# One more Strassen pair in a fused attention and feed-forward kernel, with two loads issued later

## The chip, the cores and the metric

The kernel runs on one core of a Trainium2 chip. The core has five engines that work side by side, each through its own queue in order: TensorE (PE in the profile; its weight loads are PEld), VectorE (DVE), ScalarE (ACT), GpSimd (POOL) and SyncE (SP), which here only issues transfers. Transfers issued by SP run in the DMA queue q1, those issued by POOL in q0. The time is that of one execution on the device in microseconds (us); the figure for a kernel is the median of its runs.

## The reference

Two steps. First attention with a local window and a few global keys, for 4 batches of 8 heads, 768 positions and 64 features:

```python
scores = scale * np.matmul(q, k.transpose(0, 1, 3, 2))
keep = is_global | is_local            # key < 8, or 0 <= query - key < 96
bias = -slopes[:, None, None] * dist   # distance, capped for the global keys
a = softmax(np.where(keep, scores + bias, -1e9))
x = matmul(a, v)                       # as 3072 tokens of 512 features
```

Then a feed-forward layer over the 3072 tokens, with 1536 inner features:

```python
gate = np.maximum(x @ w_gate, 0.0)
val = x @ w_val
out = gate * val @ w_out
```

Inputs and output are float32; the kernel computes in bfloat16 and accumulates in float32.

## The kernel before

**Halves and stages.** Each batch is cut into two halves of 384 queries, so there are eight halves, numbered 0 to 7 (the third half is number 2, the fourth number 3). For each half the kernel computes attention, which gives the tile `xT` (512 features by 384 tokens), and then the feed-forward layer. The feed-forward of half `c` is stage `c`; while it runs, the attention of half `c + 1` is woven between its matmuls. Halves 0 and 1 are treated apart at the start: stages 0 and 1 come in a hand-written order (the string at L812), and the loop at L866 makes stages 2 to 7.

**A stage.** `ffn_pieces(c)` (L598) returns two lists. `f1` has 24 blocks: for each of 12 chunks of 128 inner features a `gate` and a `val`, four matmuls of 384 columns each (L607). ACT rectifies the gate block (L614, tile `grelu`), DVE multiplies the val block with it (L620, tile `ht`). Both read PSUM banks of the pool `ff`, which has three. `f2` makes the output. The 384 tokens of a half are three tiles of 128 tokens, and there are two ways to make their output rows:

- plain, `outp` (L622): 12 matmuls of 512 columns for one tile (L627), then one ACT copy (L632) and one store (L633);
- as a pair of tiles, `winograd` (L512): Winograd's form of Strassen's scheme, with seven products m1 to m7 of six matmuls of 256 columns (L549) for two tiles, where eight would be the plain number. It needs four sums s1 to s4 of the two tiles' `ht` (`add`, L535 on DVE) and four sums t1 to t4 of `wo_sb`, made once (`wo_sum`, L842). The results are joined with ACT copies (L566, L578, L581, L584) and DVE additions (L569, L574, L588, L589). s2 needs s1, and s4 needs s2.

Tiles 0 and 1 of a half always form a pair from half 1 on. The third tile is plain, except in the halves of `PAIRED` and the ones after them: there the third tiles of both form a further pair, whose seven products run at the start of `f2` of the second half.

**Sums.** The sums are split in first and second halves over the 12 chunks (chunks 0 to 2 and 3 to 5 of the lower six, with their partners). The first halves are made behind certain `val` blocks (`behind`, L646), the second halves between the products (`rest`, `places`, L648 and L678).

**Attention.** `attention_pieces(s)` (L493) lists 26 pieces for four pairs of heads: the scores of a pair (`pair_scores`, L397 on PE, four banks of the pool `x`, which has five), the exps (L406 on ACT), the masks (L359 on DVE), the products with v for each head (`piece_av`, L427 on PE, then a logarithm L436 and, after the second head, a reciprocal L441 on ACT), and the norms that write `xT` (`piece_norm`, L446 on DVE). `early_pieces(s)` (L377) come a stage earlier: POOL casts k and q to bfloat16 (L363, tile `kqc`), SP transposes them by DMA (L368, tile `kqT`), and the keys are copied into their order in `kT` (L259 to L265).

**What sets the order.** The schedule is manual: every engine gets its instructions in program order. `spread` gives a list of pieces positions between two shares of a stage, and `weave` (L689) emits each piece after the first block at which the stage's done share, counted in the blocks' nominal weights (0.65 each), has reached its position.

**The loads at the start.** `load_qk_after(s)` (L161) writes one element of `qs` and `ks` (L166) and then issues the two loads on SP (L113): the loads wait for the memsets. For half 2 the memsets are on DVE. `more` (L810) calls it behind `K0`, and calls `loads` (group 2 of the gate and val weights, then `wo_sb`, on POOL, L155, and some memsets) behind `S20`. At L852 POOL copies one element of `wo_sb` into `held` before the last cast of half 2, so that this cast waits for `wo_sb`. Half 2's `kT` copies are on POOL for the pairs 0 and 1 and on ACT for the pairs 2 and 3 (L374).

Of the kernel before, what the change touches and what calls it, by code (L numbers as in the profile page):

```python
# [15 lines left out]
def kernel(  # L16
# [50 lines left out]
    early, first = ExitStack(), ExitStack()  # L67
# [39 lines left out]
    def load_qk(s, h0, h1):  # L107
        b, half = divmod(s, 2)
        if s not in qs_of:
            qs_of[s] = late["stage"].tile([128, H, NN * D], FP32, name="qs")  # L110
            ks_of[s] = late["stage"].tile([128, H, NN * D], FP32, name="ks")
        for src, dst in ((k, ks_of[s]), (q, qs_of[s])):
            nc.sync.dma_start(  # L113
                out=dst[:, h0:h1, :],
                in_=src[b, h0:h1, half * QH : (half + 1) * QH, :].rearrange(
                    "h (p n) d -> p h (n d)", n=NN))
# [28 lines left out]
    def load_v_half(s):  # L145
        b, half = divmod(s, 2)
        if half == 0:
            load_v_globals(b)
            if s != 2:
                spread_v_globals(b)  # L150
        for j in range(4) if half == 0 else range(4, NT):
            load_v(b, j)

    def load_w(dst, src, f0, f1):
        nc.gpsimd.dma_start(out=dst, in_=src[:, f0:f1].rearrange("(c p) f -> p c f", p=128))  # L155

    def load_w_group(i):
        load_w(wg[i], moe_w_gate, i * GW * 128, (i + 1) * GW * 128)
        load_w(wv[i], moe_w_val, i * GW * 128, (i + 1) * GW * 128)

    def load_qk_after(s, eng=nc.vector):  # L161

        qs_of[s] = late["stage"].tile([128, H, NN * D], FP32, name="qs")
        ks_of[s] = late["stage"].tile([128, H, NN * D], FP32, name="ks")
        for t in (qs_of[s], ks_of[s]):
            eng.memset(t[0:1, 0:1, 0:1], 0.0)  # L166
        load_qk(s, 0, H)
# [209 lines left out]
    def early_pieces(s):  # L377
        out = [(0.0, lambda p=p, i=i: piece_cast(s, p, i)) for i in range(2) for p in range(HP)]
        out += [(0.0, lambda n=n: piece_x(s, n)) for n in range(NN)]
        out += [(0.0, lambda p=p: piece_order(s, p)) for p in range(HP)]  # L380
        return out
# [111 lines left out]
    def attention_pieces(s):  # L493
        QK = lambda p: [(0.15, lambda g=g: piece_qk(s, p, g)) for g in range(3)]
        AV = lambda p: [(0.29, lambda e=e: piece_av(s, p, e)) for e in range(2)]
        N = lambda p: [(0.0, lambda: piece_norm(s, p))]
        g = QK(3)
        a = AV(2)
        gap = [(0.0, lambda: None)] * (2 if s == 2 else 1)
        return (QK(0) + QK(1) + AV(0) + N(0) + gap + QK(2) + AV(1) + N(1) + gap  # L500
                + g[0:1] + a[0:1] + g[1:2] + a[1:2] + g[2:3] + N(2) + AV(3) + N(3))
# [90 lines left out]
        return add, [(0.65, (m1, m2, m3, m4, m5, m6, m7)[i - 1]) for i in order]  # L592


    PAIRED = (4, 6)
    third_of = {}

    def ffn_pieces(c):  # L598
# [36 lines left out]
        def begin():  # L635
            two = psum["s"].tile([128, 2, 512], FP32, name="s_ps")
            st["g", 1], st["v", 1] = two[:, 0], two[:, 1]
            for d0, d1 in ((0, 2), (2, N_DC - 1)):
                for key, w in (("g", wg), ("v", wv)):
                    for fc in range(2):  # L640
                        product(w, key, fc, d0, d1)

        plain = range(NN) if c < 1 else () if c - c % 2 in PAIRED else (NN - 1,)
        add, products = winograd([(c, ht, 0), (c, ht, 1)], "sums", (1, 5, 6, 4, 7, 2, 3) if c == NHALF - 1 else
                                 (1, 2, 5, 6, 4, 3, 7) if c in PAIRED else (1, 5, 4, 6, 2, 3, 7))
        behind = {2: [lambda: add(3, 0, 3)], 7 if c == 2 else 5: [lambda: add(3, 3, 6)], 8: [lambda: add(1, 0, 3)],  # L646
                  9: [lambda: add(2, 0, 3)], 10: [lambda: add(4, 0, 3)]}
        rest = tuple(lambda j=j: add(j, 3, 6) for j in (1, 2, 4))  # L648
        if c in PAIRED:
            third_of[c] = ht  # L650
        elif c - 1 in PAIRED:
            add3, products3 = winograd([(c, ht, NN - 1), (c - 1, third_of[c - 1], NN - 1)], "sums3",
# [23 lines left out]
        elif c > 1:  # L676
            f2 += (products3 if c - 1 in PAIRED else []) + products
            places = (2, 3, 5) if plain else (0, 1, 2) if c in PAIRED else (0, 1, 2, 3)  # L678
            for at, f in list(zip(places, rest))[::-1]:
# [4 lines left out]
    def spread(items, first, last):  # L684

        n = len(items)
        return [(first + (i + 0.5) / n * (last - first), f) for i, (_, f) in enumerate(items)]

    def weave(f_items, *placed):  # L689
        total = sum(t for t, _ in f_items)  # L690
        a_items = sorted((x for p in placed for x in p), key=lambda x: x[0])
        done, ai = 0.0, 0
        for t, f in f_items:
            f()
            done += t
            while ai < len(a_items) and a_items[ai][0] * total <= done:
                a_items[ai][1]()
                ai += 1
        for _, f in a_items[ai:]:
            f()  # L700
# [95 lines left out]
    def Z():  # L796
        for p in range(HP):
            nc.gpsimd.memset(kT[1][p][:, 3, 32:128].bitcast(mybir.dt.uint32), 0)
            nc.gpsimd.memset(kT[1][p][:, 6, NG + 48 : 128].bitcast(mybir.dt.uint32), 0)
# [5 lines left out]
    def loads():  # L805
        load_w_group(2)
        load_w(wo_sb, moe_w_out, 0, DM)
        Z()

    more = {"K0": lambda: load_qk_after(2), "S20": loads}  # L810
    begin_of[0][0]()
    for f in ("m0 g0 g1 v0 m3 K3 m2 g2 m1 v1 K2 v2 S30 K0 S31 K1 S21 g3 S20 v3 S01 A3 N3 S00 S11 "  # L812
              "g6 g7 A2 S10 g4 v7 A0 N2 v4 v6 A1 N0 N1 g5 v5").split():
# [52 lines left out]
    for c in range(2, NHALF):  # L866
        placed = []
        if c + 2 < NHALF:
            load_qk(c + 2, 0, H)
            load_v_half(c + 2)  # L870
            placed.append(spread(early_pieces(c + 2), 0.25, 0.75))
        if c + 1 < NHALF:
            pieces = ahead.pop(c + 1, None) or attention_pieces(c + 1)
            if c in PAIRED:

                placed.append([(0.76, pieces[-2][1]), (0.84, pieces[-1][1])])
                placed.append(spread(pieces[:-2], 0.05, 0.7))
            else:
                placed.append(spread(pieces, *(0.07, 0.82) if c == 2 else (0.0, 0.8)))
        if c + 1 in PAIRED:  # L880
            ahead[c + 2] = attention_pieces(c + 2)
            placed.append(spread([ahead[c + 2].pop(0) for _ in range(3)], *(0.885, 0.975) if c - 1 in PAIRED else (0.82, 0.93)))
        f1, f2 = ffn_pieces(c)
        weave(f1 + f2, *placed)
# [35 lines left out]
```

## Time and profile before

| what | us |
|---|---|
| median of 3 runs | 239.0 (238.91 to 239.96) |
| the profiled execution's time | 238.84 |
| its span, first to last instruction | 237.0 |
| TensorE busy | 231.0 |
| VectorE busy | 171.5 |
| ScalarE busy | 156.4 |
| GpSimd busy | 88.7 |

The profile is that of one execution. Its page has the busy time of each engine, the span in 40 slices, the DMA queues, the chain of work that ended last (followed back from the last instruction, at each step to what released it) and the costliest groups of instructions. A row of busy time by window has: the window in us, its length, then for PE, PEld, DVE, ACT and POOL the busy time and the number of instructions, the granted TensorE clock (1.00 is full), the DMA share and GB/s. A row of a timeline has the start in us, the busy time, engine, line, operation, output and input, form and count; in brackets stands how long the engine had been idle and what released it. A row of the chain has start, length and what ran. A row of a DMA queue has packets, MB and the time that its packets took as a share of 16 engines' time; since packets overlap, it can pass 100%.

### The profile page before, as it was taken

Reading aid. Unit: us, or ns where it says so; the run is one execution under the profiler, and the core shown is the slowest. Engines: PE = TensorE matmul, PEld = TensorE weight load, DVE = VectorE, ACT = ScalarE, POOL = GpSimd, SP = SyncE. Lnnn points to the kernel's source line nnn. Section 1 sums busy time; section 2 is a strip of 40 time slices with the busy share of each in tenths; the row PEclk is TensorE's granted clock in tenths of the full one; section 3 lists DMA queues with packets and bytes.
Section 4 is the critical chain, followed back from the end, with each engine's and each line's share of the span. In section 5 each row is a group of like instructions: output and inputs, shape, how many; then the busy total and the mean of one; then the engine's idle time right before and its main releaser. Section 6 shows DMA issues by size and latency. Waiting matters only on the chain.

```text
span 237.0 us, 5436 instructions
## 1 busy us (share of the span) xinstructions
PE 231.0 (97%) x1981; PEld 149.5 (63%) x1981; DVE 171.5 (72%) x460; ACT 156.4 (66%) x358; POOL 88.7 (37%) x204
## 2 busy tenths in 40 slices
PE   7999999999999999999999999999999999999994
PEld 2655565565576566766668666856588666866683
DVE  7885965868847778666787677868985777956652
ACT  5996973437786777757877678567786578534330
POOL 6795894217434944604185060913260000000000
PEclk9999999999999999999999999999999999999999
DMA  6999999994997995757609947096522200020022
GB/s 203 191 166 175 235 260 218 195 155 66 284 202 175 288 150 110 56 154 244 118 16 125 248 134 133 2 202 206 94 43 88 91 0 0 4 88 0 3 81 97
DMA packets 70515, 31.42 MB, mean 133 GB/s; under 512 B 47176, under 2 KB 67400, under 8 KB 70488
## 3 DMA queue, kind: packets, MB, share of 16 engines
q0 software_dynamic: 32800, 8.71, 36.5%
q1 hardware_dynamic: 36472, 21.45, 34.4%
q10 hardware_dynamic: 1216, 0.92, 1.2%
q8 instruction: 15, 0.25, 0.4%
q14 instruction: 12, 0.10, 0.1%
HBM read 28.41 MB, written 6.29 MB: 146 GB/s over the span
## 4 chain that ended last, share of the span: by engine, by line
PE 87%; DMA 9%; POOL 1%; DVE 1%; issue 0%; SPq 0%
PE ff_ps L607 52%; PE ff_ps L549 12%; DMA wg<-in_moe_w_gate_dram 7%; PE ff_ps L627 7%; PE x_ps L427 6%; PE x_ps L549 5%; PE x_ps L397 4%; DMA kq<-in_k_dram 2%; PE t_ps L459 1%; POOL kq L744 1%; PE s_ps L459 0%; POOL wv L155 0%; POOL wg L155 0%; DVE qk L281 0%; SPq L182 0%
## 5 line engine op out<-in xcount | busy, mean ns | idle before, releaser
L607 PE MATMUL ff_ps<-xT,wg 128*128 128x384 bf16 x380 | 77.7, 326 | 0.4 <-DMA wg<-in_moe_w_gate_dram 0.4
L607 PE MATMUL ff_ps<-xT,wv 128*128 128x384 bf16 x380 | 77.6, 326 | 0.0
L620 DVE TENSOR_TENSOR ht<-ff_ps,grelu 128x384 bf16<-128x384 f32 x95 | 52.8, 556 | 31.7 <-PE ff_ps L607 20.6
L614 ACT ACTIVATE grelu<-ff_ps 128x384 bf16<-128x384 f32 x95 | 46.4, 490 | 43.0 <-PE ff_ps L607 20.3
L607 PEld LDWEIGHTS <-wg 128*128 128x128 bf16 x384 | 36.1, 98 | 23.8 <-issue 0.8
L607 PEld LDWEIGHTS <-wv 128*128 128x128 bf16 x384 | 35.8, 98 | 22.9
L406 ACT ACTIVATE es<-x_ps 128x360 bf16<-128x360 f32 (+2 forms) x96 | 35.6, 448 | 2.6 <-PE x_ps L397 2.6
L359 DVE TENSOR_TENSOR es<-es,m_all 128x432 bf16<-128x432 bf16 (+4 forms) x108 | 28.6, 316 | 5.1 <-ACT es L406 5.0
L446 DVE TENSOR_TENSOR xT<-x_ps,rcp 64x384 bf16<-64x384 f32 x48 | 26.6, 554 | 6.6 <-ACT rcp L441 5.9
L436 ACT ACTIVATE lnd<-x_ps 64x384 f32<-64x384 f32 x48 | 23.3, 485 | 10.7 <-PE x_ps L427 10.0
L363 POOL CAST kqc<-ks 128x384 bf16<-128x384 f32 x24 | 11.9, 542 | 32.1 <-DMA ks<-in_k_dram 32.1
L549 PEld LDWEIGHTS <-s 128*128 128x128 bf16 x216 | 21.0, 98 | 2.4
L427 PE MATMUL x_ps<-es,vbuf 128*128 128x216 bf16 (+4 forms) x216 | 21.8, 225 | 0.0
L137 POOL DMA_DIRECT2D vbuf<-in_v_dram x25 | 21.6, 877 | 0.2
L549 PE MATMUL ff_ps<-t,s 128*128 128x256 bf16 x162 | 21.6, 273 | 0.0
L427 PEld LDWEIGHTS <-vbuf 128*128 128x128 bf16 x216 | 15.8, 97 | 6.4
L627 PE MATMUL ff_ps<-wo_sb,ht 128*128 128x512 bf16 x72 | 17.7, 379 | 0.0
L549 PEld LDWEIGHTS <-ht 128*128 128x128 bf16 x162 | 15.4, 98 | 2.7 <-DVE xT L446 0.2
L363 POOL CAST kqc<-qs 128x384 bf16<-128x384 f32 x24 | 11.7, 527 | 8.2 <-DMA qs<-in_q_dram 8.2
L263 POOL COPY kT<-kqT 128x240 bf16<-128x240 bf16 x16 | 6.8, 424 | 20.9 <-DMA kqT<-kqc 18.5
L535 DVE TENSOR_TENSOR s<-ht 128x384 bf16<-128x384 bf16 (+1 forms) x34 | 13.1, 386 | 0.8
L441 ACT ACTIVATE rcp<-lnd 128x384 f32<-128x384 f32 x24 | 12.6, 523 | 0.8
(118 smaller groups left out, 246.2 us busy)
## 6 DMA issues: line engine op xcount, KB each, us to landing
out_dram<-osb SPq DMA_DIRECT2D x23, 256.0 KB, 2.3
ks<-in_k_dram SPq DMA_DIRECT2D x6, 768.0 KB, 5.5
qs<-in_q_dram SPq DMA_DIRECT2D x6, 768.0 KB, 12.2
vbuf<-in_v_dram POOLq DMA_DIRECT2D x21, 120.0 KB, 7.4
wo_sb<-in_moe_w_out_dram POOLq DMA_DIRECT2D x1, 1536.0 KB, 19.8
wg<-in_moe_w_gate_dram POOLq DMA_DIRECT2D x2, 512.0 KB, 9.6
wv<-in_moe_w_val_dram POOLq DMA_DIRECT2D x2, 512.0 KB, 11.4
wg<-in_moe_w_gate_dram POOLq DMA_DIRECT2D x2, 256.0 KB, 6.4
```

Source lines behind the costliest of these rows:

```text
L137: nc.gpsimd.dma_start(out=v_dst(b, NG + r0, NG + r0 + n, j), in_=v[b, :, KT * j + r0 : KT * j + r0 + n, :].rearrange("h p d -> p h d"))
L359: nc.vector.tensor_mul(for_all, for_all, mk)
L363: nc.gpsimd.tensor_copy(kqc[:, :, i].rearrange("t n (h d) -> t h n d", d=D)[:, 2 * p : 2 * p + 2], of[s][:, 2 * p : 2 * p + 2, :].rearrang ...
L406: nc.scalar.activation(es[:, e, 0:c], banks[e][:, 0:c], AF.Exp, bias=0.0, scale=scale)
L427: nc.tensor.matmul(av3[:, :, a : a + w], lhsT=vb[:, j, z0 : z0 + 128], rhs=es[:, e, c : c + NN * w].rearrange("k (n p) -> k n p", n=NN), s ...
L436: nc.scalar.activation(ln[o0 : o0 + 64], av[d0 : d0 + 64, 0:QH], AF.Ln, bias=0.0, scale=1.0)
L446: nc.vector.tensor_tensor(xT_of[s][r, p, :], av_of[s, p, e][r, 0:QH], av_of[s, p, "r"][r], op=ALU.mult)
L549: nc.tensor.matmul(st[key][:, 0:D2], lhsT=left(i), rhs=right(i), start=start and i == 0, stop=i == N2 - 1, skip_group_check=not start)
L607: nc.tensor.matmul(st[key][:, 0:QH], lhsT=w_of(w, dc, fc), rhs=xT_of[c][:, dc, :], start=(dc == 0), stop=(dc == N_DC - 1))
L614: nc.scalar.activation(gr, psg[:, 0:QH], AF.Relu, bias=0.0, scale=1.0)
L620: nc.vector.tensor_tensor(ht[:, fc, :], psv[:, 0:QH], st["gr", fc], op=ALU.mult)
L627: nc.tensor.matmul(ps2, lhsT=ht[:, fc, n * 128 : (n + 1) * 128], rhs=wo_sb[:, fc, :], start=(fc == 0), stop=(fc == N_FC - 1))
```

## The change

Three edits:

- `load_qk_after(2)` moves from behind `K0` to the end of `loads`, behind `S20`.
- `PAIRED` gets the entry 2: the third tiles of halves 2 and 3 are a pair whose products run in stage 3. Stage 2 has no plain tile any more (its product order becomes 1, 2, 5, 6, 4, 3, 7, its second sum halves stand around the first two products), and stage 3 has seven more products instead of its plain tile.
- The attention of half 3, woven into stage 2, was spread over 7 to 82 per cent of the stage; now all but its last two pieces are spread over 7 to 80 per cent, and the last value piece stands at 80.5, the last norm at 83.5 per cent. In the stages 4 and 6 the figures stay 5 to 70, 76 and 84. In stage 3 the first three pieces of half 5 move from 82 to 93 to 88.5 to 97.5 per cent, since the stage before is now in `PAIRED`.

```diff
-    PAIRED = (4, 6)
+    PAIRED = (2, 4, 6)
...
         load_w(wo_sb, moe_w_out, 0, DM)
+        load_qk_after(2)
         Z()
 
-    more = {"K0": lambda: load_qk_after(2), "S20": loads}
+    more = {"S20": loads}
...
             if c in PAIRED:
 
-                placed.append([(0.76, pieces[-2][1]), (0.84, pieces[-1][1])])
-                placed.append(spread(pieces[:-2], 0.05, 0.7))
+                first, until, av, norm = (0.07, 0.8, 0.805, 0.835) if c == 2 else (0.05, 0.7, 0.76, 0.84)
+                placed.append([(av, pieces[-2][1]), (norm, pieces[-1][1])])
+                placed.append(spread(pieces[:-2], first, until))
             else:
-                placed.append(spread(pieces, *(0.07, 0.82) if c == 2 else (0.0, 0.8)))
+                placed.append(spread(pieces, 0.0, 0.8))
```

## The prediction

> **What bounds the kernel now.** I read the page, then the busy time of each engine by stage (a stage is one half's feed-forward, `c` in the code), then the chain that ended last, then the timelines of the two places that the change touches, and there the DMA queues. The page, parts 1 and 4:
>
> ```profile
> span 237.0 us, 5436 instructions
> PE 231.0 (97%) x1981; PEld 149.5 (63%) x1981; DVE 171.5 (72%) x460; ACT 156.4 (66%) x358; POOL 88.7 (37%) x204
> ...
> PE 87%; DMA 9%; POOL 1%; DVE 1%; issue 0%; SPq 0%
> ```
>
> Stages 2, 3, 4 and 5 one after the other:
>
> ```profile
> 75.76:103.04 27.28, 27.28 (x231) 17.85 (x230) 19.54 (x50) 19.96 (x46) 16.23 (x36) 1.00 0.97 145
> 103.04:130.46 27.42, 27.42 (x226) 17.65 (x224) 20.52 (x53) 20.14 (x49) 11.50 (x25) 1.00 0.72 133
> 130.46:154.77 24.31, 24.31 (x211) 16.50 (x209) 18.31 (x47) 17.21 (x40) 10.08 (x23) 1.00 0.55 128
> 154.77:184.34 29.57, 29.56 (x255) 20.54 (x254) 23.74 (x61) 21.05 (x52) 7.96 (x21) 1.00 0.56 125
> ```
>
> Length and PE busy agree in each row: TensorE never waits here, at full clock. So matmul time saved shortens the span, and so does every new wait of PE lengthen it. Stages 4 and 5 already have the form that 2 and 3 are to get. The chain in stage 2's tail (start, length, what):
>
> ```profile
> 95.26 1.94 PE ff_ps L627 x9
> ...
> 97.51 0.65 PE ff_ps L627 x3
> 98.15 0.30 PE x_ps L427 x5
> 98.46 1.31 PE ff_ps L549 x12
> ```
>
> A 512-column matmul of the plain tile costs 0.65/3 = 0.217 us, a 256-column one of a pair 1.31/12 = 0.109.
>
> **Part 1, the Strassen pair, on PE.** Stage 2 loses a plain tile: 12 x 0.217 = -2.60. Stage 3 loses one as well and gains seven products of six matmuls: 42 x 0.109 = 4.59, so +1.99; by the two stage rows (29.57 against 27.42) +2.15. I take +2.10. The rest of stage 3 I cost at nothing: its ten more DVE instructions (four sums of about 0.38, two of 0.6, four additions of 0.42: 4.4 us) and two more copies on ACT make it stage 5's mix, where 23.74 of DVE and 21.05 of ACT hide under PE. Half 2's third store moves on SP from 98.80 into stage 3; k and q of half 5 (104.25) then stand behind two stores instead of three, and half 4's transposes (86.41) stay ahead of all: nothing. Sum so far -0.50.
>
> **Part 2, stage 2's tail.** The plain tile's 2.60 us, which the change takes out, stood between the last `val` and the first product of the pair, and DVE used it. T is the end of the last `val`. In the changed kernel's order the last pair of heads is scored with five gate or val blocks left (now three), and pair 2's norms stay behind the last `val`'s multiplication and ahead of the second halves of the sums s1, s2, s4.
> - ACT: now, the reciprocal of pair 2 ends 4.50 after the last scores begin (92.11 to 96.61). From there to T lie 0.41 of scores, five blocks of 0.65, a switch of 0.11 and two value pieces of 0.30: 4.37. It ends at T+0.1, and the last rectification (0.49), which now ran 94.34 to 94.83, ahead of it, ends at T+0.6.
> - PE: m1 takes the bank that this frees: T+0.65 to 1.3 instead of T. Two value pieces to 1.9, m2 to 2.6.
> - DVE: multiplication (0.56) to T+1.2, norms (1.14) to 2.3, s1 (0.36) to 2.7, s2 to 3.05.
> - m5 wants s1: 2.75 to 3.4; m6 to 4.05, m4 to 4.7. On DVE m2's addition (0.42) ends at 3.5, pair 3's norms at 4.65, s4 at 5.0. m3 wants s4: 5.05 to 5.7; m7 ends at 6.4.
>
> Unhindered it would be 0.60 + 4.59 = 5.2: PE waits 1.2. If ACT were in time the same sums give 0.75; in stage 4, whose norms of pair 2 stand before the last `val`, it is 0. Before the tail half 3's pieces move one or two blocks forward, at no cost: the tightest distance, from pair 0's last value piece to pair 2's scores, which want the bank that its norm frees (86.43, scores at 86.44), stays three blocks. I take 1.2, since each link is a row and the order is fixed; the ends 0 and 1.4 stay for the range. xT of half 3 is done at T+4.7, before stage 3 begins.
>
> **Part 3, k and q of half 2.** The two memsets move on DVE behind the masks of S20, from 24.50 to about 27.1, and SP's two issues with them from 24.67 to about 27.3. Nothing on SP stands behind them until 48.59; POOL's order is the same. So they go out behind the weights of group 2 (26.62, 27.36) but before wo (28.10). What each queue moved from 24.6 to 27.5, from 28 to 31 and from 31 to 36:
>
> ```profile
> q0 software_dynamic: 585, 0.58, 122.9%
> ```
> ```profile
> q1 hardware_dynamic: 1128, 0.86, 88.6%
> q0 software_dynamic: 123, 0.11, 22.5%
> ```
> ```profile
> q0 software_dynamic: 661, 0.66, 78.1%
> q1 hardware_dynamic: 642, 0.48, 38.8%
> ```
>
> q1, SP's queue, moved nothing until 27.5 although it had its work at 24.67. So PE's one wait for weights (0.36 at 27.59) is not its doing, and I credit no gain. Then k went alone (1128 packets in 3 us), then q shared with wg, wv and wo, packet for packet. What waits at the far end (POOL's timeline, then ACT's):
>
> ```profile
> 42.47 1.41 POOL L363 CAST kqc<-qs 128x384 bf16<-128x384 f32 x3 [4.28 <-DMA qs<-in_q_dram]
> 47.95 0.18 POOL L852 COPY held<-wo_sb 1x1 bf16<-1x1 bf16 x1 [4.07 <-DMA wo_sb<-in_moe_w_out_dram]
> 48.07 0.50 POOL L363 CAST kqc<-qs 128x384 bf16<-128x384 f32 x1
> 55.05 0.54 POOL L259 COPY kT<-kqT 128x360 bf16<-128x360 bf16 x1 [6.48 <-DMA kqT<-kqc]
> ```
> ```profile
> 55.13 0.54 ACT L259 COPY kT<-kqT 128x360 bf16<-128x360 bf16 x1
> ...
> 57.14 1.34 ACT L406 ACTIVATE es<-x_ps 128x240 bf16<-128x240 f32 x4
> 58.69 1.36 ACT L406 ACTIVATE es<-x_ps 128x240 bf16<-128x240 f32 x4 [0.20 <-PE x_ps L397]
> ```
>
> q has 4 us of slack, because the last cast waits for wo. wo has nearly none: kqT lands at 55.0 and ACT takes it at 55.13; behind that copy stand a rectification and the exps of pair 0, whose banks pair 1's scores want at 58.37. If the last cast comes X later, PE waits about X - 0.35. X is 0 if the queues do the same work in another order. At the other end k shares from 28.3 on: 1024 packets at 642/5 = 128 per us are 8 us, then q as now 11.4 (31.0 to 42.4), so 47.7; three casts, the check on wo and the last cast (2.1) make 49.8 against 48.57: X = 1.3. Nearest is the row from 28 to 31, k alone, begun up to a us later: some 400 packets fall into the shared time, where one costs q0 1/128 - 1/205 = 0.0029 us (205 per us: q0 alone, 508 packets from 42.5 to 45), so wo lands 1.1 later, less what q0 moves while k starts up. I take X = 0.65, a wait of 0.3; ends 0 and 0.95.
>
> The Trainium skill, "DMA: Bandwidth & Descriptors", section "Queues, rings and completion order", says that each DMA engine goes round robin between the queues that have work, packet by packet. The row from 31 to 36 agrees, the row from 28 to 31 does not show it. By the rule k and q would share from the start, and the sum below would be 0.65 higher.
>
> A second page speaks against the pair itself: the Trainium skill, "TensorE: Matmul & The Clock Gate", section "Back-to-back issue gap", gives about 131 ns for a 512-column matmul in a stream with weight loads. The pair would then save at most 24 x 0.131 = 3.1 us and lose. The rows say 217 ns, and the measurement decides.
>
> **Sum.** -2.60 + 2.10 + 1.20 + 0.30 = +1.0 on the profiled execution's 238.84 us (237.0 of span, 1.8 around it): 239.84. The median of the runs, 239.0, is 0.16 above that execution: 240.0.
>
> **Rivals.**
> - *The tail does not wait* (the other side). Place: s1 at the end of stage 2. It decides if s1's second half is ready by m5, 1.9 us after T, and s4 by m3. For it: stages 4 and 5 run the same product orders without a wait. Against: there the norms of pair 2 stand earlier. Price -1.2, and k and q at nothing: 238.84 - 0.50 + 0.16 = 238.5. With the 0.36 wait for weights gone too, 238.1.
> - *k and q share from the start* and come behind wo: the wait is 0.95 instead of 0.3, 240.65; with the tail at 1.4, 240.9. For it: the row from 31 to 36, and wg's group 2, now issued first. Against: k ran alone once it had begun.
> - *All of stage 2 is short of ACT*: 19.96 - 0.58 us of it in about 25 instead of 27.3. If each of the four pairs' scores waited for one exp more (0.39), that is 1.6: 241.6. Against: ACT would be 78% busy, DVE in stage 5 is 80% without a wait.
>
> **Numbers.** Forecast 0.50, tail does not wait 0.22, sharing 0.20, ACT 0.08. The range goes from the first rival's low end to the sharing with its long tail, 240.9, and 0.4 more for the spread of the runs (238.91 to 239.96); it leaves out the ACT case: 238.1 to 241.3. The forecast's own is 239.5 to 240.5. A measurement of this kernel tells about 0.5%, 1.2 us, from no change. Slower than 240.2: 0.18 of the forecast (a wait of 1.4, or X of 1), nearly all of the sharing (0.18) and the ACT case (0.08): 0.44. Below 237.8 only a first rival with more gain than I find, 0.07. Same: 0.49.
>
> **What would show it.** Right: stage 2 about 25.8 us long with PE idle in its last 6.5, released by DVE's L535 and ACT's L614; stage 3 about 29.5, all PE; k's issue at 27.3; a PE wait at L397 near 57 to 59 of some 0.3. Wrong: stage 2 near 24.7 and all busy; or kqT landing at 55.0 as now; or PE waiting in the middle of stage 2; or the wait at 27.59 gone.

## The result and the profile after

The changed kernel takes 240.22 us (median of 18 runs, 239.88 to 242.91), the kernel before 239.0 us (18 runs beside them, 238.25 to 240.25): 1.0056 times as long, with a 95% interval of 1.0039 to 1.0072, so about 1.3 us slower. The first profile of the changed kernel is of an execution of 242.91 us, which is not typical (the next longest run is 240.92): TensorE waits 2.59 us there for the keys of half 2, and behind that wait the granted clock is 0.50 from 60 to 63 us. The lines here are from a second profile, of 240.33 us at full clock. Its page, parts 1 and 4:

```profile
span 238.6 us, 5481 instructions
PE 230.9 (97%) x1996; PEld 151.5 (64%) x1999; DVE 174.2 (73%) x470; ACT 156.4 (66%) x360; POOL 89.4 (37%) x204
...
PE 76%; DMA 13%; DVE 4%; SPq 2%; POOL 1%; ACT 1%; issue 1%; POOLq 0%; ACTq 0%
```

TensorE is busy as long as before (231.0), although its matmuls are 0.61 us less (2.60 saved, 1.99 paid), and the span is 1.6 us longer (237.0): waits were added, and part of them lies inside the busy time. The chain that ended last now has 4% on DVE and 13% on DMA, where it had 1% and 9%. Stages 2 and 3 (stages 4 and 5 are 24.38 and 29.42 long, all PE, against 24.31 and 29.57):

```profile
77.21:102.63 25.42, 25.04 (x220) 16.50 (x218) 19.74 (x50) 19.17 (x45) 16.42 (x37) 1.00 1.01 145
102.63:132.04 29.41, 29.41 (x256) 20.56 (x254) 23.54 (x61) 21.04 (x52) 12.13 (x25) 1.00 0.71 134
```

Stage 2 lost 1.86 us (27.28 before) where its matmuls lost 2.60; stage 3 gained 1.99 (27.42 before), and PE never waits there. Together +0.13. Stage 2 is the one of the four whose PE time is shorter than its length. The chain in its tail:

```profile
96.67 0.48 ACT grelu L614
...
97.17 0.56 DVE ht L620
97.73 0.46 DVE xT L446
...
98.20 0.57 DVE xT L446
...
98.79 0.37 DVE s L535
...
99.57 0.42 DVE osb L569
100.00 0.46 DVE xT L446
...
101.06 0.37 DVE s L535
```

From the last rectification to the last sum the chain is nearly all DVE: multiplication, norms of pair 2, s1, m2's addition, norms of pair 3, s4. PE in the same place (the products m5 and m6, then m3, then m7; the next stage starts at 102.47):

```profile
98.46 0.49 PE L549 MATMUL ff_ps<-t,s 128*128 128x256 bf16 x3
99.21 1.16 PE L549 MATMUL ff_ps<-t,s 128*128 128x256 bf16 x9 [0.26 <-DVE s L535]
...
100.86 1.12 PE L549 MATMUL ff_ps<-wo_sb,s 128*128 128x256 bf16 x6
101.81 0.82 PE L549 MATMUL ff_ps<-t,s 128*128 128x256 bf16 x6
```

Read by starts, since the ends are modelled: three matmuls of m5 take 0.33, so m5's fourth would start at 98.79 and starts at 99.21, 0.42 late; m3's six take 0.95 instead of 0.65, 0.30 late. The wait inside m3 has no bracket.

The loads of half 2 at the far end, on POOL, and PE behind them:

```profile
48.58 1.41 POOL L363 CAST kqc<-qs 128x384 bf16<-128x384 f32 x3 [5.73 <-DMA qs<-in_q_dram]
49.96 0.18 POOL L853 COPY held<-wo_sb 1x1 bf16<-1x1 bf16 x1
50.08 0.50 POOL L363 CAST kqc<-qs 128x384 bf16<-128x384 f32 x1
57.01 0.65 POOL L259 COPY kT<-kqT 128x360 bf16<-128x360 bf16 x1 [6.43 <-DMA kqT<-kqc]
```
```profile
58.03 0.45 PE L397 MATMUL x_ps<-kqT,kT 64*128 64x216 bf16 x8 [0.87 <-POOL kT L261]
```

Before, q's casts began at 42.47 and the copy to `held` waited for `wo_sb`; now q comes last, the copy waits for nothing, and PE waits 0.87 us for the keys of half 2. The same two places of PE before, the wait for `wg` and the scores without a wait:

```profile
27.59 1.47 PE L607 MATMUL ff_ps<-xT,wg 128*128 128x384 bf16 x8 [0.36 <-DMA wg<-in_moe_w_gate_dram]
...
56.59 0.45 PE L397 MATMUL x_ps<-kqT,kT 64*128 64x216 bf16 x8
```

The wait for `wg` is not there in the changed kernel's second profile, but this execution comes to that place half a microsecond later (28.10).

### The profile page after: what moved, and what is told of

Read it like the earlier page. It is cut to its first block, busy times and chain, and to the rows that moved or that the text cites. A ratio compares the mean times of both kernels' runs of the same rounds, so it can differ in the third digit from the quotient of the medians.

```text
span 241.1 us, 5481 instructions
## 1 busy us (share of the span) xinstructions
PE 232.3 (96%) x1996; PEld 151.7 (63%) x1999; DVE 175.9 (73%) x470; ACT 156.4 (65%) x360; POOL 88.8 (37%) x204
## 4 chain that ended last, share of the span: by engine, by line
PE 78%; DMA 13%; DVE 3%; POOL 1%; ACT 1%; SPq 1%; issue 1%; ACTq 0%; POOLq 0%; DVEq 0%
PE ff_ps L607 41%; PE ff_ps L549 13%; DMA qs<-in_q_dram 9%; PE x_ps L427 5%; PE x_ps L549 5%; PE ff_ps L627 5%; PE x_ps L397 4%; DMA kq<-in_q_dram 3%; DMA kqT<-kqc 1%; PE t_ps L310 1%; SPq L368 1%; PE s_ps L341 1%; POOL kqc L363 1%; PE t_ps L272 1%; DVE xT L446 1%; PE t_ps L459 1%
## 5 line engine op out<-in xcount | busy, mean ns | idle before, releaser
L607 PE MATMUL ff_ps<-xT,wg 128*128 128x384 bf16 x380 | 77.7, 326 | 0.0
L607 PE MATMUL ff_ps<-xT,wv 128*128 128x384 bf16 x380 | 77.6, 326 | 0.0
L614 ACT ACTIVATE grelu<-ff_ps 128x384 bf16<-128x384 f32 x95 | 46.4, 489 | 43.1 <-PE ff_ps L607 22.3
L607 PEld LDWEIGHTS <-wg 128*128 128x128 bf16 x384 | 36.3, 98 | 23.1 <-issue 0.9
L607 PEld LDWEIGHTS <-wv 128*128 128x128 bf16 x384 | 35.7, 98 | 23.2
L359 DVE TENSOR_TENSOR es<-es,m_all 128x432 bf16<-128x432 bf16 (+4 forms) x108 | 30.7, 337 | 4.9 <-ACT es L406 4.9
L446 DVE TENSOR_TENSOR xT<-x_ps,rcp 64x384 bf16<-64x384 f32 x48 | 26.5, 553 | 3.8 <-ACT rcp L441 3.2
L549 PEld LDWEIGHTS <-s 128*128 128x128 bf16 x240 | 23.2, 98 | 3.7 <-DVE s L535 1.1
L549 PE MATMUL ff_ps<-t,s 128*128 128x256 bf16 x180 | 24.1, 273 | 0.4 <-DVE s L535 0.4
L427 PE MATMUL x_ps<-es,vbuf 128*128 128x216 bf16 (+4 forms) x216 | 21.6, 225 | 0.0
L427 PEld LDWEIGHTS <-vbuf 128*128 128x128 bf16 x216 | 15.8, 97 | 5.5
L549 PEld LDWEIGHTS <-ht 128*128 128x128 bf16 x180 | 17.1, 98 | 2.7 <-DVE xT L446 0.2
L363 POOL CAST kqc<-qs 128x384 bf16<-128x384 f32 x24 | 12.9, 574 | 11.1 <-DMA qs<-in_q_dram 11.1
L535 DVE TENSOR_TENSOR s<-ht 128x384 bf16<-128x384 bf16 (+1 forms) x37 | 15.0, 405 | 0.8
L397 PE MATMUL x_ps<-kqT,kT 64*128 64x216 bf16 (+4 forms) x216 | 11.3, 227 | 2.6 <-POOL kT L261 2.6
```

Of the source, the lines that this page charges most:

```text
L359: nc.vector.tensor_mul(for_all, for_all, mk)
L363: nc.gpsimd.tensor_copy(kqc[:, :, i].rearrange("t n (h d) -> t h n d", d=D)[:, 2 * p : 2 * p + 2], of[s][:, 2 * p : 2 * p + 2, :].rearrang ...
L397: nc.tensor.matmul(banks[e][:, c : c + NN * w].rearrange("k (n t) -> k n t", n=NN), lhsT=kt[r, j, :], rhs=qd[r, :, a : a + w], start=True, ...
L427: nc.tensor.matmul(av3[:, :, a : a + w], lhsT=vb[:, j, z0 : z0 + 128], rhs=es[:, e, c : c + NN * w].rearrange("k (n p) -> k n p", n=NN), s ...
L446: nc.vector.tensor_tensor(xT_of[s][r, p, :], av_of[s, p, e][r, 0:QH], av_of[s, p, "r"][r], op=ALU.mult)
L549: nc.tensor.matmul(st[key][:, 0:D2], lhsT=left(i), rhs=right(i), start=start and i == 0, stop=i == N2 - 1, skip_group_check=not start)
```

## The experiments

Ratios are to the kernel before, run on the same chip (238.75 us median for the first four kernels, 238.57 for the others).

### The changed kernel once more

> The changed kernel once more, since its profile on record is of an execution 2.7 us above the median of its runs. Theory (two costs, one gain): 240.2 us; stage 2 some 25.6 us long with PE waits that add up to about 0.9 to 1.2 in its last 6.5 us, stage 3 at 29.4, and at the first scores of half 2 (L397) a PE wait of 0.3 to 1.0 us. Rival (late k and q are nearly all of it): the wait at L397 is again about 2.6 us, as in the profile on record, and the tail of stage 2 costs less than the pair saves.

Measured: 240.12 us, 1.0056 (1.004 to 1.0072). The result repeats to the fourth digit; this is the profile shown above. Stage 2 (25.42) and its waits (0.72) are a little below what was expected (25.6, 0.9 to 1.2), and the wait at L397 is 0.87, where the rival wanted 2.6.

### Only the loads moved

```diff
         load_w(wo_sb, moe_w_out, 0, DM)
+        load_qk_after(2)
         Z()
-    more = {"K0": lambda: load_qk_after(2), "S20": loads}
+    more = {"S20": loads}
```

> The kernel before with the two loads of half 2 moved behind S20 and nothing else. Theory: the last cast of half 2 comes 0.65 us later, PE waits 0.3 (up to 0.95): 239.3 us, at most 240.0. Rival (late k and q are nearly all of it): q lands after wo, the last cast comes 2 us later or more, PE waits 1.5 or more: 240.5 or more. Second rival (hidden): 239.0.

Measured: 239.68 us, 1.0037 (1.0019 to 1.0056). What the two queues moved from 28 to 31 and from 31 to 36 us:

```profile
q0 software_dynamic: 453, 0.45, 106.0%
q1 hardware_dynamic: 69, 0.05, 7.3%
```
```profile
q0 software_dynamic: 652, 0.64, 75.9%
q1 hardware_dynamic: 649, 0.50, 39.4%
```

SP issued k at 27.12, 0.67 us behind the issue of group 2's `wg` (26.45). In the first stretch k hardly moved (69 packets, against 1128 before), and the two queues together moved 0.50 MB where they had moved 0.97. From 31 on they share packet for packet, and go on so: 789 to 786 from 36 to 42. k never has the engines alone. On POOL and PE:

```profile
48.21 1.41 POOL L363 CAST kqc<-qs 128x384 bf16<-128x384 f32 x3 [5.92 <-DMA qs<-in_q_dram]
...
49.69 0.50 POOL L363 CAST kqc<-qs 128x384 bf16<-128x384 f32 x1
56.70 0.53 POOL L259 COPY kT<-kqT 128x360 bf16<-128x360 bf16 x1 [6.51 <-DMA kqT<-kqc]
```
```profile
57.60 0.45 PE L397 MATMUL x_ps<-kqT,kT 64*128 64x216 bf16 x8 [1.33 <-POOL kT L261]
```

The last transfer of the group lands 0.26 later than before (q at 48.21, against `wo_sb` at 47.95). But the one that lands last is now q, with three casts (1.41) ahead of the last one, where it was `wo_sb`, with none. The last cast starts 1.62 later (48.07 to 49.69), the copy into `kT` 1.65 later, and PE waits 1.33. The wait lies between the theory's upper end (0.95) and the rival's 1.5. In this execution the 0.36 for `wg` is gone, which makes +0.97 by the two traces; the ratio says +0.88 (0.45 to 1.34). That the moved loads are what removes the wait for `wg` is not shown: in a later kernel with both loads late ("The loads late, and wo later still") PE waits 0.48 for it. Nor is the wait at L397 the same in each execution: with both loads late it is 0.87, 1.33 and 2.59 in three profiles, and 0.47 in one with the loads in their place (that of "Only the norms of pair 2 later").

### Only the pair, the loads back in their place

```diff
         load_w(wo_sb, moe_w_out, 0, DM)
-        load_qk_after(2)
         Z()
-    more = {"S20": loads}
+    more = {"K0": lambda: load_qk_after(2), "S20": loads}
```

(against the changed kernel)

> The pair of the third tiles of halves 2 and 3 with the new positions of half 3's attention; the loads of half 2 stay where they were. Theory: -0.5 for the pair and +1.2 for the waits in stage 2's tail, 239.7 us. Rival (late k and q are nearly all of it): -0.5 to -0.2, 238.5 to 238.8.

Measured: 239.0 us, 1.0013 (0.9993 to 1.0033), which is +0.3 us, between the theory (+0.7) and the rival (-0.2). The two parts alone add to 1.0050, against 1.0056 together. PE in the tail of stage 2, then ACT's last rectification:

```profile
95.36 0.82 PE L549 MATMUL ff_ps<-wo_sb,ht 128*128 128x256 bf16 x6
...
98.04 1.16 PE L549 MATMUL ff_ps<-t,s 128*128 128x256 bf16 x9 [0.27 <-DVE s L535]
...
100.36 0.50 PE L549 MATMUL ff_ps<-wo_sb,s 128*128 128x256 bf16 x3 [0.18 <-DVE s L535]
...
101.36 0.81 PE L607 MATMUL ff_ps<-xT,wg 128*128 128x384 bf16 x4
```
```profile
95.49 0.47 ACT L614 ACTIVATE grelu<-ff_ps 128x384 bf16<-128x384 f32 x1
```

m1 starts at 95.36, right behind the last `val`, although the last rectification runs from 95.49 to 95.96: m1 does not wait for the bank that this frees. Which bank it takes the trace does not name. Both waits fall on the fourth matmul of a product, because the first three use the first half of the sum. From m1 to the next stage it is 6.00, of which 5.20 are work: 0.80 of waits.

### The norms placed later on DVE

```diff
+                if c == 2:
+                    norm = 0.865
-                placed.append(spread(pieces[:-2], first, until))
+                at = spread(pieces[:-2], first, until)
+                if c == 2:
+                    at[22] = (0.79, at[22][1])
+                placed.append(at)
```

On top of the kernel with the pair alone: the norms of pair 2 stand behind s1's second half, those of pair 3 behind s4.

> As the run with the pair alone, but on DVE in stage 2's tail the norms of pair 2 stand behind the second half of s1 and those of pair 3 behind that of s4. Theory: m5 no longer waits for s1 nor m3 for s4, m1 still waits 0.65 for the rectification: 0.55 us faster than the run with the pair alone, 239.15. Rival (the tail's waits come from ACT's order alone): the same as the run with the pair alone, within 0.15.

Measured: 238.65 us, 0.9992 (0.9973 to 1.001). Stage 2:

```profile
76.21:101.08 24.87, 24.87 (x220) 16.59 (x219) 19.79 (x50) 19.15 (x45) 16.26 (x36) 1.00 0.96 145
```

The row is 0.62 us shorter than with the norms where the change has them (25.49). The tail is 5.38, with 0.18 left at m6, which wants s2. So most of the waits in the tail are the place of the norms in DVE's order. The times agree but don't show it alone: the intervals of this kernel and of the one with the pair alone overlap. The theory's other half, that m1 waits 0.65 for the rectification, did not come true.

### Only the norms of pair 2 later

```diff
                 if c == 2:
-                    norm = 0.865
+                    norm = 0.835
```

(against the kernel just before)

> e3 with one move: the norms of pair 2 behind s1's second half on DVE; those of pair 3 stay ahead of s4. Theory (each norm costs the wait of the product behind it): m5's wait (0.43) goes, m3's (0.34) stays, the tail is 5.6 us and the time 0.9995 of before. Rival (DVE's work up to s4 is one queue, so the last sum in it is ready no earlier): m5 stops waiting, and m3 waits about 0.75 instead; the tail stays 6.0, the time 1.001 as in e3.

Measured: 239.04 us, 1.0009 (0.9988 to 1.003). The times can't tell the theories apart; PE's timeline does:

```profile
97.86 1.65 PE L549 MATMUL ff_ps<-t,s 128*128 128x256 bf16 x12
...
100.88 0.50 PE L549 MATMUL ff_ps<-wo_sb,s 128*128 128x256 bf16 x3 [0.39 <-DVE s L535]
```

m5 no longer waits, but m3's fourth matmul starts at 100.88 instead of 100.33, 0.55 late where it was 0.34, and m6 is 0.17 late for s2. From m1 (95.94) to the next stage (101.88) it is 5.94, against 6.00. The rival holds in what the tail takes, though m3 waits 0.55 and not 0.75: DVE's work up to s4 is one queue, and moving a norm inside it only moves the wait to the next products.

### Both norms placed by the spread instead

```diff
-                first, until, av, norm = (0.07, 0.8, 0.805, 0.835) if c == 2 else (0.05, 0.7, 0.76, 0.84)
+                first, until, av, norm = (0.07, 0.77, 0.805, 0.865) if c == 2 else (0.05, 0.7, 0.76, 0.84)
```

(against the kernel with the pair alone)

> The changed kernel with the loads of half 2 back behind K0, the norms of pair 2 placed on DVE ahead of the last val's multiplication (last value piece 0.805, spread of the others up to 0.77) and those of pair 3 behind s4 (0.865). Theory (the tail of stage 2 waits only because norms stand on DVE between the second halves of the sums): no PE wait from m1 to m7, the tail 5.2 us as its matmuls add up, against 6.0 in e3 and 5.4 in e4; stage 2 24.7 us all PE, stage 3 29.41; the sum is -2.60 + 1.99 = -0.6 against before, so 0.9975 of it, about 238.2 to 238.5. Rival (the denser attention earlier in stage 2 leaves ACT short, or the wait moves to another product): stage 2 25.0 or longer with PE idle ahead of the tail at L607 or L427, and the time equals before or e3, 1.000 to 1.001.

Measured: 239.44 us, 1.0035 (1.0017 to 1.0053). From m5 on no product waits in the tail, as the theory has it, but stage 2 is 25.44 long by PE's starts (75.68 to 101.12), as long as with the waits. The chain in the last third of stage 2 shows where they went:

```profile
88.79 0.32 PE x_ps L427 x5
...
89.13 0.49 ACT lnd L436
...
89.64 0.53 ACT rcp L441
...
90.20 0.56 DVE xT L446
...
90.80 0.31 PE x_ps L397 x3
```

The last pair's scores want the bank that pair 1's norm frees. Spread up to 0.77 instead of 0.8, they stand two blocks behind pair 1's value piece instead of three (1.71 us by starts, 88.62 to 90.33, against 2.35 with the norms moved by hand), and the chain value piece, logarithm, reciprocal, norm takes longer than that. The scores take 0.72 instead of 0.41, the value piece ahead of m1 0.59 instead of 0.31. PE's timeline shows no idle time at either: it lies inside the busy time. What the value piece ahead of m1 waits for is not shown. The rival was right that the wait moves to another place, but it expected PE idle at L607 or L427 and a time of at most 1.001, which is exceeded.

> The kernel of e5 once more, beside e4's. Its profile lost 0.56 us more in stage 2 than e4's (25.44 against 24.88): the last pair's scores took 0.72 instead of 0.41 and the last value piece but one 0.59 instead of 0.31, both for banks of x or exps that ACT had not finished. By that, e3's stage length (25.49), the time is e3's: 1.001 of before, and 1.0035 was partly the spread of the runs. If it comes out at 1.003 or more again, the packing costs more in most executions than in the profiled one.

> The kernel of e4 once more, beside e5's: norms of pair 2 behind s1's second half, those of pair 3 behind s4, loads of half 2 behind K0. If its gain over e3 is the tail's waits (0.80 us in e3, 0.18 in e4) and no accident of the runs, stage 2 is 24.9 us again and the time is 0.998 to 1.000 of before. If e4's and e5's times differ by accident (each 12 or 8 runs), the two come out alike here.

Measured, side by side on another chip: the spread 239.38 us, 1.0033 (1.0013 to 1.0052), with stage 2 at 25.45; the norms moved by hand 238.37 us, 0.9985 (0.9965 to 1.0005), with stage 2 at 24.86. Both repeat. Stage 2 differs by 0.59 us; the ratios differ by 0.0048, 1.1 us, of which the profiles show only half. Where the rest lies is open: the intervals end at 1.0005 and begin at 1.0013, so the true difference may be much smaller, and the executions profiled of the spread (239.12 and 239.25 us) are both quicker than the medians of their runs (239.44 and 239.38).

### The loads one step later, and only q late

```diff
-    more = {"K0": lambda: load_qk_after(2), "S20": loads}
+    more = {"K1": lambda: load_qk_after(2), "S20": loads}
```

> Before with one edit: the two loads of half 2 behind K1 instead of K0, so that SP issues them about 1.2 us later (near 25.9 instead of 24.7) but still ahead of the weights of group 2 on POOL's queue (26.6). Theory (what matters is which queue has its work first when the weights of group 1 end): q1 again moves about 1100 packets from 28 to 31 and q0 about 120, q lands near 42.5, kqT at 55.0, and the time is that of before, 0.999 to 1.001. Rival (each us of delay costs its share): 1.2 of 2.6 us of delay, so half of the wait seen in e2, PE waits 0.6 at L397 near 57 and the time is 1.0015 to 1.0025 of before.

Measured: 238.87 us, 1.0007 (0.9997 to 1.0018). SP's issue is at 25.77, 1.1 us later than before, and from 28 to 31 the queues moved:

```profile
q1 hardware_dynamic: 1196, 0.91, 95.0%
q0 software_dynamic: 68, 0.06, 12.5%
```

k goes alone as before. In this execution PE waits 0.50 at L397, since the transposes landed 0.3 later although the last cast was earlier (47.52), and the wait for `wg` is gone; the two nearly cancel. The ratio lies in the theory's range, though the wait is near the rival's 0.6; but the rival has it from a later cast, and here the cast was earlier.

```diff
+    def load_one(of, src, name):
+        of[2] = late["stage"].tile([128, H, NN * D], FP32, name=name)
+        nc.vector.memset(of[2][0:1, 0:1, 0:1], 0.0)
+        nc.sync.dma_start(out=of[2], in_=rows_of(src, 2, 0, H))
+
+    def loads_and_q():
+        loads()
+        load_one(qs_of, q, "qs")
+
-    more = {"K0": lambda: load_qk_after(2), "S20": loads}
+    more = {"K0": lambda: load_one(ks_of, k, "ks"), "S20": loads_and_q}
```

> Before with one edit: k of half 2 stays behind K0, only q's memset and load move behind S20 (issue near 27.3). Theory (k's start alone is what the change loses; q shared with the weights from 31 us on already): q1 moves about 1100 packets from 28 to 31, k lands 10 us after its issue as before, q near 42.5, no new wait at L397, 0.999 to 1.001 of before. Rival (q's late issue costs as well): q casts later than 44.5, the last cast later than 48.6, a PE wait at L397 above 0.5 and the time 1.002 or more.

Measured: 238.77 us, 1.0005 (0.9994 to 1.0016). q, issued at 27.38 (27.12 is where the other kernel issues k), costs nothing that shows. From 28 to 31, and then the casts:

```profile
q1 hardware_dynamic: 948, 0.72, 71.7%
q0 software_dynamic: 213, 0.21, 42.3%
```
```profile
41.90 1.41 POOL L363 CAST kqc<-qs 128x384 bf16<-128x384 f32 x3 [3.61 <-DVE ht L620]
...
47.99 0.50 POOL L363 CAST kqc<-qs 128x384 bf16<-128x384 f32 x1
```

So what the moved loads lose is k's stretch alone on the DMA engines, and it is lost between an issue at 25.8 and one at 27.1: when group 2's `wg` (issued at about 26.5) is ahead of it. A kernel with k alone late was not run.

### The loads late, and wo later still

```diff
-        load_w(wo_sb, moe_w_out, 0, DM)
+        load_qk_after(2)
...
-    more = {"K0": lambda: load_qk_after(2), "S20": loads}
+    more = {"S20": loads}
...
+    load_w(wo_sb, moe_w_out, 0, DM)
...
-    for f in (*casts[:7], lambda: nc.gpsimd.tensor_copy(held, wo_sb[0:1, N_FC - 1, 0:1]),
+    for f in (*casts[:7], lambda: None,
```

`wo_sb` is loaded behind the v loads of half 2, and the last cast does not wait for it.

> Before with the two loads of half 2 behind S20 (as in e2), but wo issued on POOL behind the v loads of half 2, some us later, and without the copy of one element of wo into held, so that the last cast waits for q alone. Theory (k and q are late because they share with wg, wv and wo, packet for packet, to the end): with wo behind them in time q shares only with wg and wv and lands some 2 to 4 us earlier than in e2 (48.2), the last cast is no later than before (48.6), PE waits nothing or little at L397 near 57, and the time is that of before, 0.999 to 1.001; if wo then lands late, its sums on DVE near 50.7 wait for it instead. Rival (the late issue itself, not the sharing, makes q late): q casts at 48.2 again, PE waits 1.3 at L397 and the time is 1.0035 to 1.004.

Measured: 242.74 us, 1.0173 (1.0147 to 1.0198). POOL, SP, DVE and PE (twice), and the busy times from 56 to 59 us:

```profile
42.41 1.86 POOL L363 CAST kqc<-qs 128x384 bf16<-128x384 f32 x4 [1.47 <-DMA qs<-in_q_dram]
57.51 0.97 POOL L259 COPY kT<-kqT 128x360 bf16<-128x360 bf16 x1 [13.24 <-DMA kqT<-kqc]
```
```profile
44.29 11.09 SPq L368 DMA_TRANSPOSE kqT<-kqc  x3
```
```profile
55.25 0.56 DVE L842 TENSOR_TENSOR t<-wo_sb 128x768 bf16<-128x768 bf16 x1 [4.11 <-DMA wo_sb<-in_moe_w_out_dram]
```
```profile
27.92 1.47 PE L607 MATMUL ff_ps<-xT,wg 128*128 128x384 bf16 x8 [0.48 <-DMA wg<-in_moe_w_gate_dram]
...
56.33 1.44 PE L607 MATMUL ff_ps<-xT,wg 128*128 128x384 bf16 x4 [3.25 <-DVE ht L620]
```
```profile
56.00:59.00 3.00, 2.67 (x9) 1.28 (x9) 2.04 (x5) 0.49 (x1) 1.50 (x4) 0.50 0.65 107
```

As to q the theory holds: with `wo_sb` loaded later, q is cast from 42.41 on, 5.8 us earlier than with the loads alone moved. But the time is lost elsewhere. The three transposes, issued at 44.29, now run beside `wo_sb` and hold SP 11.09 us instead of 4.54, so the keys come later than ever (57.51), and DVE waits 4.11 for `wo_sb` with the multiplications of two blocks queued behind it, so that PE waits 3.25. Behind that wait the granted clock is 0.50 from 56 to 59 us, and a block of four matmuls takes 1.23 to 1.28 us by starts instead of 0.65 (56.33 to 57.56 to 58.84). The expectation named DVE's wait and gave it no price. In the other kernels the copy to `held` keeps the transposes apart from `wo_sb`.

## Why the prediction was right or wrong

The time was predicted at 240.0 us and came out at 240.22, inside the forecast's own range. But two of its terms were off in opposite directions, the tail 0.4 to 0.5 too high and k and q 0.6 to 0.7 too low, and a rival's mechanism was at work in one of them. That the sum came out so near is partly luck.

| step | predicted | measured |
|---|---|---|
| stage 2 loses a plain tile | -2.60 | -2.41 to -2.42 with 0.18 of wait left (24.87 and 24.86) |
| stage 3 | +2.10 | +1.99 |
| waits in stage 2's tail | +1.20 | +0.72 (both parts), +0.80 (pair alone) |
| k and q | +0.30 | +0.97 by the two traces, +0.88 by the ratio (loads alone) |
| sum | +1.0 | +1.0 to +1.2 by these steps (with -2.60 for the plain tile), +1.3 by the ratio (0.9 to 1.7) |

- **The pair on PE** was right. Of the two figures for stage 3, the count of matmuls (+1.99) was exact, and the rest of that stage did hide under PE; the average with the stage rows (2.10) only made it worse.
- **The tail: the place was right, the size too large.** With T the end of the last `val` (96.54), DVE did what was worked out to a tenth: the rectification ended at T+0.6, the multiplication at T+1.2, the norms at T+2.2 (2.3 predicted), s1 at T+2.6 (2.7), s4 at T+4.9 (5.0). The step that failed is "m1 takes the bank that this frees: T+0.65": in the kernel with the pair alone, m1 starts 0.13 before the last rectification does. And m5 and m3 were taken to want their sum at their start, where they want its second half at their fourth matmul, 0.33 later. The next stage came at T+5.9 instead of T+6.4. The text's 0.75 for the case "ACT in time" is near the 0.72 measured, but ACT was no earlier than forecast; m1 did not need it. The rival without a wait in the tail was wrong, but its ground was right: the norms standing behind the sums is what the wait is.
- **k and q: the mechanism of the rival came true in the main.** The step that failed is "Nearest is the row from 28 to 31, k alone, begun up to a us later". k did not run alone later; it shared from its first packets, and at first it got far less than half (69 packets to 453). X itself passed the upper end that was set (1.3), because k also started later: it reached an even share only near 31. The relation "PE waits about X - 0.35" fits in number (X = 1.65, wait 1.33), but not in its reason: it was worked out for pair 1's scores behind ACT's exps, and PE waits for pair 0's keys from POOL, which it reaches 0.4 us earlier than before in this execution. Against the kernel before the loss is 0.97, which is X - 0.68. By the rule of the Trainium skill, "DMA: Bandwidth & Descriptors", section "Queues, rings and completion order", the two queues share packet by packet while both have work; the rows from 31 us on agree (652 to 649, 789 to 786). The wait for `wg` (0.36), credited with nothing, is gone in the profiles of the changed kernel and of the loads alone, and the text had named that as a sign of being wrong. The runs don't settle it: the wait is 0.48 in a kernel with both loads late, absent in the one with the loads one step later, and absent in executions that come to this place late. By the ratio the net cost (0.88) is near that of the rival as priced (0.95).
- **The signs named beforehand**: stage 2 (25.42, forecast 25.8) and stage 3 (29.41, all PE) are as forecast, and with the loads alone k is issued at 27.12 (27.3). The waits in the tail are released by DVE's L535, none by ACT's L614, and the wait at L397 is 0.87 and 1.33 where 0.3 was named.
- **ACT in stage 2** was no bound: the kernel with the norms moved has it at 19.15 of 24.87 us and loses 0.18.
- The 131 ns for a 512-column matmul in a stream with weight loads (the Trainium skill, "TensorE: Matmul & The Clock Gate", section "Back-to-back issue gap") is not what this kernel shows: with that figure, by an estimate, stage 2 would have lost at most 1.6 us (12 x 0.131), and it lost 2.42 with the waits moved away.

No version here beats the kernel before by more than its measurement tells. The pair with the norms moved behind the sums, and the loads left alone, comes nearest (0.9992 and 0.9985): 2.60 saved, 1.99 paid, 0.18 waited.

## What to carry to other kernels

When a change takes out work that an engine used as slack, write down the queue of the next engine up to the last result that is needed, and compare that sum with the products in front of it; moving one item within this queue moved the wait here, and moving the items behind the results that are needed removed most of it. Moving them ahead of the queue removed it too, and cost as much earlier in the stage. When a load is issued later, ask which transfer it now stands behind at the moment when the DMA engines come free, and what work is left after the one that lands last: here 2.2 us of delay for q alone cost nothing that the runs tell, and 2.5 us for k and q together cost about 0.9 us.

## What was not expected of the hardware

- When the transfers of two queues begin close together, one queue can have most of the engines' time for some 3 us: k, issued at 24.67, moved nothing until 27.5 and then 1128 packets against 123 from 28 to 31; issued at 27.12 it moved 69 against 453. The sharing packet for packet came only afterwards. The start is not a fixed time behind the issue: k issued at 24.82 (only q late) and at 25.77 (the loads one step later) had moved 5 packets each by 27.5, while the other queue was busy with weights. Why the first queue keeps its lead was not told apart.
- A long wait of TensorE cost more than itself in the two profiles that have one: behind the waits of 2.59 us (the changed kernel's first profile) and 3.25 us (the loads late, wo later) the granted clock was 0.50 for 2.5 to 3 us, and behind those of 0.87 and 1.33 us it stayed at 1.00.
- Time that TensorE waits can lie inside its busy time: the stage with the scores 0.31 late has 25.35 of 25.45 us busy, and the same work takes 24.86. A stage's busy share near 100% is no proof that nothing waits; the starts of the blocks are.
- Three transposes by DMA next to a plain load held SP 11.09 us instead of 4.54 (one profile, with the loads late and wo later).
- The first 12 us vary between executions of the same program: PE waits for its first keys up to 1.14 us there, in kernels whose code is the same up to that point:

```profile
12.18 0.43 PE L341 MATMUL s_ps<-kqT,kT 64*128 64x216 bf16 x8 [1.14 <-DVE kT L260]
```

(the kernel with the norms moved, first profile; the wait is 0.69 in its second and absent before). A comparison of two profiles' spans carries that much that is not the change's.
